# Attention and a gated feed-forward on one core: another plan of issue, transfers in parts, another order of the first steps

## The chip, the core and the metric

The kernel runs on one core of one Trainium2 chip. TensorE (PE), VectorE (DVE), ScalarE (ACT) and GpSimd (POOL) each work through their own queue of instructions in order. SyncE (SP) issues all the transfers, in order too. The metric is the device time of one execution in microseconds.

## The reference

There are 8 batches of 8 heads, 1152 keys and values of 64 numbers each, and queries that are averaged in pairs, so 576 per head. The attention's output, heads side by side, is the token matrix x of a gated feed-forward.

```python
q_pool = q.reshape(B, H, S // 2, 2, D).mean(axis=3)
scores = scale * np.matmul(q_pool, k.transpose(0, 1, 3, 2))
attn = np.exp(scores - np.max(scores, axis=-1, keepdims=True))
x = (attn / (attn.sum(-1, keepdims=True) + 1e-09)) @ v     # heads joined: B x 576 x 512
xk = mu_k * x + (1.0 - mu_k) * x_prev                       # x_prev: the token before
xr = mu_r * x + (1.0 - mu_r) * x_prev
k = np.maximum(xk @ w_k, 0.0)
out = 1.0 / (1.0 + np.exp(-(xr @ w_r))) * (k * k @ w_v)
```

## The kernel before

**Work.** A head's 576 queries are taken as 6 blocks of 96, 384 blocks in all. A block is a chain over four engines. PE multiplies 9 pieces of keys (`ks1`) by the block's queries into one of three score tiles `s` (L391). DVE takes a maximum over the pieces, `mx` (L398), PE turns it (L401), DVE takes it over the rest, `mb` (L404), PE spreads it (L406), and ACT writes it as one more row into the low half of the turned queries `qT` (L409). Nine products with `ks2` add the low halves and subtract the maximum (L415). ACT takes exp into `pf` (L421), POOL cuts out its low half `pl` (L423). Windows of 128 queries are then multiplied by the values `vt` and `vb` (L441, L443, L448).

**Preparation.** Every operand is split into a high and a low float16 half. For each head, `prep` loads `kr` and `vr` (L339), makes `kn` (ACT L346, DVE L348), turns it with a transposing transfer into `ks1` (L352), copies half of that to `ks2` (L354), and makes `vt` and `vb`. For each pair of heads, `queries` loads `qr` (L315), adds neighbours into `qs` (L319), makes the high and low halves of `qn` (ACT L322, DVE L326) and turns them into `qT` with one transposing transfer (L329). `qr`, `qs` and `qn` have one buffer, `qT` has two. `weights` loads 20 tiles into `st` (L499) and converts each with three operations on DVE (L511, L512, L514), two on ACT and one on POOL. A load of keys or values is 288 KB, of queries 576 KB, of a weight tile 512 KB.

**Feed-forward.** Tiles of 256 tokens. `mix` makes `xk` and `xr` from the tokens `xt` and the vectors `mu` and `omu` = 1 - mu (L549, L552, L557). PE multiplies by the weights (L577). The first such tile can start when batch 0, the first 48 blocks, is done.

**The order of work.** All of this is first recorded in a list: engine, planned duration, what is read and written. `Issue.run` then plays the list with these durations (`play`), engine by engine, in 1 + 6 rounds, keeps the order of the round with the shortest planned total, and writes the instructions in that order. Each engine later follows its own order, whatever the real times are. Transfers are one engine, "DMA", with a planned issue time (0.82 for a load, 1.01 for `ks1`, 1.9 for `qT`, 1.46 for a weight tile) and a fixed 2.0 from there to landing. Everything that stands ahead of the list (constants, memsets, `mu`) is ordered by the framework.

Of the kernel before, what the change touches and what calls it, by code (L numbers as in the profile page):

```python
# [19 lines left out]
P = 128  # L20
# [25 lines left out]


class Issue:
# [20 lines left out]
    def add(self, eng, dur, fn, r=(), w=(), key=0.0, port=None):  # L69
# [23 lines left out]
        self.ops.append((eng, dur, fn, key, deps, eng == "POOL" if port is None else port))  # L93
# [79 lines left out]
    def run(self, wait, rounds=6):  # L173
# [11 lines left out]
        start, total = self.play(eng, dur, pred, succ, [o[3] for o in ops], wait, port)  # L185
        best = (total, start)
        for _ in range(rounds):
            fin = [-(start[n] + dur[n]) for n in range(N)]
            back, _ = self.play(eng, dur, succ, pred, fin, wait, port)
            pr = [-(back[n] + dur[n]) for n in range(N)]  # L190
            start, total = self.play(eng, dur, pred, succ, pr, wait, port)
            if total < best[0]:
                best = (total, start)
        start = best[1]
        for n in sorted(range(N), key=lambda n: (start[n], n)):
# [4 lines left out]
def kernel(  # L200
# [109 lines left out]
    def queries(n, key):  # L310
# [18 lines left out]
        op("DMA", 1.9, lambda: nc.sync.dma_start_transpose(qT[i].rearrange("p r j x -> p (r j) x"),  # L329
                                                           qn[0].rearrange("p r j x -> p (r j x)")),  # L330
           r=[(m, j0) for m in ("qn", "qnl") for j0, _ in JS],
           w=[(m, i, hh, jj) for m in ("qT", "qTl") for hh in (0, 1) for jj in range(NB)], key=key + 2)

    def prep(n, key):
# [3 lines left out]
        def dma(o, src, buf):  # L338
            op("DMA", 0.82, lambda: nc.sync.dma_start(o, src), w=[buf], key=key - 2 * NB * PER)  # L339
# [3 lines left out]
        for c0, c1 in ((0, 5), (5, NC)):  # L343
# [21 lines left out]
        op("POOL", NC * D * 0.0009 + 0.066, lambda: nc.gpsimd.tensor_scalar(  # L365
# [6 lines left out]
    def block(n, j, i, t):  # L372
# [5 lines left out]
        kh, kl = ("qT", qi, hp, j), ("qTl", qi, hp, j)  # L378
# [332 lines left out]
```

## Time and profile before

| | |
|---|---|
| median of 3 runs | 1202.83 us (1202.06 to 1205.6) |
| profiled execution, its span | 1203.16 us, 1201.2 us |
| busy in the span: PE, DVE, ACT, POOL | 1133.2, 926.0, 834.6, 518.2 us |
| transfers: bytes, share of the 16 engines | 126.66 MB, 44.2% for the kernel's own queue |

The time of an execution lies some 2 us above its span, which goes from the first to the last instruction. A busy figure is the union of an engine's instructions. That PE is busy for 94% of the span is a mean over a start with hardly any work for it and a long rest in which it hardly stops, so stages are read apart below.

### The profile page before, as it was taken

What the parts mean: (1) busy time and instruction counts of PE and PEld (TensorE: products, weight loads), DVE (VectorE), ACT (ScalarE), POOL (GpSimd) and SP (SyncE); (2) the same over time, 40 slices, a digit from 0 to 9 for tenths busy, and PEclk for the clock granted to TensorE, in tenths of its full rate; (3) what the DMA queues carried; (4) which work ended last, traced back from release to release, by engine and by line L of the source; (5) the groups of instructions that cost most, each with busy time, mean ns of one, the idle gap of its engine ahead of it and who ended that gap; (6) DMA issues with size and microseconds to landing.
All of it is one profiled execution on the core that took longest, in us unless ns stands there. A gap on an engine that the chain in (4) does not pass through costs nothing.

```text
span 1201.2 us, 45386 instructions
## 1 busy us (share of the span) xinstructions
PE 1133.2 (94%) x19504; PEld 931.6 (78%) x19504; DVE 926.0 (77%) x1829; ACT 834.6 (69%) x1673; POOL 518.2 (43%) x547
## 2 busy tenths in 40 slices
PE   2778799999999999999999999999999999999998
PEld 2667787878788787978888887978787878888555
DVE  7798989888878778788787877886978788775431
ACT  5677777777667767677767676676767777755543
POOL 3555563534444444445444453544344444433111
PEclk9899999999999999999999999999999999999999
DMA  9676656564454443545443544545544544210000
GB/s 259 144 183 158 164 118 133 145 139 90 104 120 93 108 94 90 114 113 122 95 116 79 129 90 102 135 86 110 109 100 103 111 99 91 56 39 2 28 18 27
DMA packets 220777, 126.66 MB, mean 105 GB/s; under 512 B 156064, under 2 KB 192928, under 8 KB 220576
## 3 DMA queue, kind: packets, MB, share of 16 engines
q1 hardware_dynamic: 220576, 123.77, 44.2%
q8 instruction: 152, 2.49, 0.8%
q14 instruction: 49, 0.40, 0.1%
HBM read 67.11 MB, written 9.44 MB: 64 GB/s over the span
## 4 chain that ended last, share of the span: by engine, by line
PE 73%; ACT 10%; DMA 7%; issue 5%; DVE 5%; POOL 0%; SPq 0%; ACTq 0%; DVEq 0%; POOLq 0%
PE f L577 28%; PE s L415 10%; PE s L391 9%; PE a L448 6%; PE a L441 5%; PE a L443 5%; DMA qT<-qn 4%; PE s L577 4%; ACT pf L421 4%; PE a L577 2%; DVE mx L398 1%; PE s L401 1%; ACT qT L409 1%; PE s L406 1%; PE a L478 1%
## 5 line engine op out<-in xcount | busy, mean ns | idle before, releaser
L423 POOL TENSOR_SCALAR pl<-pf 128x864 f16<-128x864 uint16 x384 | 370.6, 965 | 463.3 <-ACT pf L421 430.6
L398 DVE TENSOR_REDUCE mx<-s 128x96 f16<-128x864 f32 x384 | 401.5, 1053 | 103.3 <-PE s L391 79.1
L421 ACT ACTIVATE pf<-s 128x864 int32<-128x864 f32 x384 | 336.7, 890 | 107.5 <-PE s L415 83.3
L391 PE MATMUL s<-qT,ks 128*128 128x96 f16 x3456 | 216.4, 207 | 33.2 <-DMA qT<-qn 17.1
L441 PE MATMUL a<-vt,pf 128*128 128x65 f16 x2880 | 235.5, 194 | 1.6 <-ACT pf L421 0.9
L443 PE MATMUL a<-vt,pf 128*128 128x64 f16 x2880 | 235.7, 194 | 0.0
L415 PE MATMUL s<-qT,ks 128*128 128x96 f16 x3456 | 214.4, 208 | 20.0 <-ACT qT L409 18.6
L391 PEld LDWEIGHTS <-ks 128*128 128x128 f16 x3456 | 184.1, 99 | 58.2 <-issue 23.2
L415 PEld LDWEIGHTS <-ks 128*128 128x128 f16 x3456 | 183.3, 99 | 48.9 <-issue 31.0
L441 PEld LDWEIGHTS <-pf 128*128 128x128 f16 x2880 | 203.9, 99 | 8.5 <-ACT pf L421 1.1
L443 PEld LDWEIGHTS <-pf 128*128 128x128 f16 x2880 | 193.8, 98 | 11.4 <-issue 0.9
L409 ACT ACTIVATE qT<-s 1x96 f16<-1x96 f32 x384 | 91.8, 242 | 108.8 <-PE s L406 98.7
L448 PE MATMUL a<-vb,pl 128*128 128x65 f16 x2880 | 154.3, 194 | 0.3 <-POOL pl L423 0.3
L404 DVE TENSOR_REDUCE mb<-s 96x1 f16<-96x128 f32 x384 | 108.5, 284 | 56.8 <-PE s L401 53.5
L577 PE MATMUL f<-xk,wk_lo 128*128 128x256 bf16 x496 | 136.9, 276 | 0.0
L577 PE MATMUL f<-xk,wk_hi 128*128 128x256 bf16 x496 | 136.6, 275 | 0.2 <-ACT r L604 0.2
L577 PE MATMUL f<-xlk,wk_hi 128*128 128x256 f16 x496 | 134.5, 271 | 0.0
L608 POOL TENSOR_TENSOR gl<-g 128x512 f16<-128x512 f32 x72 | 77.7, 1079 | 125.6 <-ACT g L606 124.2
L448 PEld LDWEIGHTS <-pl 128*128 128x128 f16 x2880 | 122.9, 99 | 4.9 <-POOL pl L423 0.4
L577 PEld LDWEIGHTS <-wk_hi 128*128 128x128 f16 x1152 | 104.8, 97 | 13.0 <-issue 0.4
L577 PE MATMUL f<-wv_hi,g 128*128 128x512 f16 x240 | 90.9, 379 | 1.1 <-ACT em L627 0.8
L577 PE MATMUL f<-wv_lo,g 128*128 128x512 f16 x240 | 90.9, 379 | 0.0
(89 smaller groups left out, 1881.7 us busy)
## 6 DMA issues: line engine op xcount, KB each, us to landing
qr<-in_q_dram SPq DMA_DIRECT2D x32, 576.0 KB, 4.7
kr<-in_k_dram SPq DMA_DIRECT2D x64, 288.0 KB, 3.2
vr<-in_v_dram SPq DMA_DIRECT2D x64, 288.0 KB, 3.0
ks<-ks SPq DMA_DIRECT2D x64, 144.0 KB, 2.7
out_dram<-em SPq DMA_DIRECT2D x36, 256.0 KB, 2.4
st<-in_moe_w_k_dram SPq DMA_DIRECT2D x8, 512.0 KB, 5.2
st<-in_moe_w_v_dram SPq DMA_DIRECT2D x8, 512.0 KB, 4.2
st<-in_moe_w_r_dram SPq DMA_DIRECT2D x4, 512.0 KB, 5.0
```

The costliest lines, as they stand in the source:

```text
L391: nc.tensor.matmul(cols(c, c + 1), ks1[hp][:, c, :], qhi, start=(c == c0), stop=False, skip_group_check=True)
L398: op("DVE", 0.967, lambda: nc.vector.tensor_reduce(mxz, grid(0, NC).rearrange("p c q -> p q c"), axis=AX.X, op=ALU.max), r=[("s", z)], w=[ ...
L404: op("DVE", 0.199, lambda: nc.vector.tensor_reduce(mbz[0:QN], s[0:QN, 0:P], axis=AX.X, op=ALU.max), r=[("s", z)], w=[("mb", z)], key=t + O ...
L409: op("ACT", 0.133, lambda: nc.scalar.activation(qlo[QN:QN + 1], s[QN:QN + 1, 0:QN], AF.Prelu, scale=1.0 - EPS, alpha=(1.0 + EPS) / (1.0 - ...
L415: nc.tensor.matmul(cols(c, c + 1), ks2[hp][:, c, :], qlo, start=False, stop=True, skip_group_check=True)
L421: op("ACT", NC * QN / 1200 + 0.051, lambda: nc.scalar.activation(pf[:, :, rows], grid(0, NC), AF.Exp, bias=SHIFT, scale=0.125 / (2.0 * SQ) ...
L423: op("POOL", NC * QN / 1000 + 0.066, lambda: nc.gpsimd.tensor_scalar(pl[:, :, rows], half(pf, U16, 0)[:, :, rows], LO, 1.0, op0=ALU.mult, ...
L441: nc.tensor.matmul(a_b[:, a0:a0 + VN], half(pf, F16, 1)[:, c, rows], vt[jv][:, c, D:D + VN], start=(w == 0 and c == 0), stop=False, skip_g ...
L443: nc.tensor.matmul(a_b[:, a0:a0 + D], half(pf, F16, 1)[:, c, rows], vt[jv][:, c, 0:D], start=False, stop=False, skip_group_check=True)
L448: nc.tensor.matmul(a_b[:, a0:a0 + VN], pl[:, c, rows], vb[jv][:, c, 0:VN], start=False, stop=(c == NC - 1), skip_group_check=True)
L577: nc.tensor.matmul(ps, terms[i][0], terms[i][1], start=(first and i == 0), stop=(i == last), skip_group_check=True)
L608: op("POOL", 2 * n * 0.0022 + 0.066, lambda f2=f2: nc.gpsimd.tensor_tensor(gl[:, f2, 0:n], g32[:, f2, 0:n], gh[:, f2, 0:n], op=ALU.subtrac ...
```

## The change

It has four parts. The planner: other durations take the place of the old ones, each transfer gets its own time from issue to landing (`tail`), every engine but PE is planned 8% slower (`LATE`) and each dependence between engines 0.1 us longer (`SLACK`), and a round's order is valued by a second pass that keeps it fixed (`follow`), over 12 rounds. The transfers: the load of `qr` and the turning of `ks1` are cut in two, the turning of `qT` in four (high and low half, pieces 0 to 4 and 5 to 8). The first steps: `mu` is recorded in the list after the first heads, the first two weight tiles wait for the first heads, two small copies of the identity move from DVE to POOL, a memset gets smaller, a one-element exp is written ahead of the list. The subtractions for keys and tokens are on DVE in both kernels.

```diff
+LATE, SLACK = 0.08, 0.1
...
-            lat = 0.0 if war and e == eng else self.lat(e, eng)
+            lat = self.ops[m][6] if e == "DMA" else 0.0 if war and e == eng else self.lat(e, eng)
...
-    def run(self, wait, rounds=6):
+    def run(self, wait, rounds=12):
...
-        dur = [o[1] for o in ops]
+        dur = [o[1] if o[0] == "PE" else o[1] * (1.0 + LATE) for o in ops]
...
+                lat += SLACK if eng[m] != eng[n] or eng[n] == "DMA" else 0.0
...
+            order = sorted(range(N), key=lambda n: (start[n], n))
+            start, total = self.follow(eng, dur, pred, succ, order, port)
+            if best is None or total < best[0]:
+                best = (total, order)
...
-    nc.vector.tensor_copy(identb, ident)
+    nc.gpsimd.tensor_copy(identb, ident)
...
-    nc.vector.tensor_scalar(negi, ident, -1.0 / SM, None, op0=ALU.mult)
+    nc.gpsimd.tensor_scalar(negi, ident, -1.0 / SM, 1.0, op0=ALU.mult, op1=ALU.mult)
...
+    nc.scalar.activation(mx[0][0:1, 0:1], identb[0:1, 0:1], AF.Exp)
...
-        nc.sync.dma_start(t_, m.rearrange("(c p) -> p c", p=P))
...
+        op("DMA", 0.46, lambda: nc.sync.dma_start(t_, m.rearrange("(c p) -> p c", p=P)), w=[("mu", n)], key=60.0)
+        op("DVE", 0.1, lambda: nc.vector.tensor_scalar(o, t_, -1.0, 1.0, op0=ALU.mult, op1=ALU.add),
...
-        op("DMA", 0.82, lambda: nc.sync.dma_start(qr[0], qv), w=[("qr",)], key=key - 2 * NB * PER)
...
+            op("DMA", 0.36, lambda js=js: nc.sync.dma_start(qr[0][:, js], qv[:, js]), w=[("qr", j0)],
+               key=key - 2 * NB * PER, tail=3.0)
...
-        op("DMA", 1.9, lambda: nc.sync.dma_start_transpose(qT[i].rearrange("p r j x -> p (r j) x"),
...
+            for r_, m, t_ in ((0, "qn", "qT"), (1, "qnl", "qTl")):
+                op("DMA", 0.14 * (j1 - j0) + 0.08, lambda js=js, r_=r_: nc.sync.dma_start_transpose(
+                    qT[i][:, r_, js], qn[0][:, r_, js].rearrange("p j x -> p (j x)")),
...
-        op("DMA", 1.01, lambda: nc.sync.dma_start_transpose(ks1[i], kn[i].rearrange("p c x -> p (c x)")),
...
+            op("DMA", 0.14 * (c1 - c0) + 0.08, lambda cs=cs: nc.sync.dma_start_transpose(
+                ks1[i][:, cs], kn[i][:, cs].rearrange("p c x -> p (c x)")),
...
-                op("DMA", 1.46, lambda s3=s3, src=wv[c, :, f:f + 512]: nc.sync.dma_start(s3, src), w=[ks], key=key)
+                op("DMA", 0.36, lambda s3=s3, src=wv[c, :, f:f + 512]: nc.sync.dma_start(s3, src),
+                   r=[("ks1", 1, 0), ("ks2", 0), ("vr", 1)] if iss.nw <= 2 else [], w=[ks], key=key, tail=4.5)
```

The change moves nearly every instruction of every queue, so three places are shown. The first is SP's queue at the start of the program, before the change:

```order
L293 DMA mu_k_132<-in_moe_mu_k_dram 128x4x1
L293 DMA mu_r_136<-in_moe_mu_r_dram 128x4x1
L315 DMA qr0_74<-in_q_dram 128x9x128
L339 DMA kr0_70<-in_k_dram 128x576
L339 DMA vr0_72<-in_v_dram 128x576
L339 DMA kr1_71<-in_k_dram 128x576
L339 DMA vr1_73<-in_v_dram 128x576
L499 DMA st1_120<-in_moe_w_k_dram 128x1024
L315 DMA qr0_74<-in_q_dram 128x9x128
L499 DMA st0_119<-in_moe_w_k_dram 128x1024
L352 DMA_TRANSPOSE ks1_0_79<-kn0_76 128x9x128
L329 DMA_TRANSPOSE qT0_83<-qn0_78 128x18x128
```

And SP's queue at the same place after it (lines of the changed kernel: L364 loads `qr`, L390 `kr` and `vr`, L340 `mu`, L404 turns `ks1`, L380 turns `qT`):

```order
L390 DMA kr0_70<-in_k_dram 128x576
L364 DMA qr0_74<-in_q_dram 128x5x128
L390 DMA kr1_71<-in_k_dram 128x576
L364 DMA qr0_74<-in_q_dram 128x4x128
L390 DMA vr0_72<-in_v_dram 128x576
L390 DMA vr1_73<-in_v_dram 128x576
L340 DMA mu_k_147<-in_moe_mu_k_dram 128x4x1
L340 DMA mu_r_149<-in_moe_mu_r_dram 128x4x1
L404 DMA_TRANSPOSE ks1_0_79<-kn0_76 128x5x128
L404 DMA_TRANSPOSE ks1_0_79<-kn0_76 128x4x128
L364 DMA qr0_74<-in_q_dram 128x5x128
L380 DMA_TRANSPOSE qT0_83<-qn0_78 128x5x128
```

Keys now come first, `mu` comes seventh and eighth, the weight tiles (`st`) stand further down, and the first turned queries are 5 pieces instead of 18.

The second place is DVE's queue after the memsets, before the change:

```order
L319 TENSOR_TENSOR qs0_75<-qr0_74 128x320
L319 TENSOR_TENSOR qs0_75<-qr0_74 128x256
L326 SCALAR_TENSOR_TENSOR qn0_78<-qs0_75,qn0_78 128x5x64
L348 TENSOR_TENSOR kn0_76<-kr0_70,kn0_76 128x5x64
L348 TENSOR_TENSOR kn0_76<-kr0_70,kn0_76 128x4x64
L254 CAST identb_66<-ident_61 128x128
L256 TENSOR_SCALAR negi_68<-ident_61 128x128
L326 SCALAR_TENSOR_TENSOR qn0_78<-qs0_75,qn0_78 128x4x64
```

And after it (L399 is the keys' subtraction, L341 makes `omu`):

```order
L399 TENSOR_TENSOR kn0_76<-kr0_70,kn0_76 128x5x64
L366 TENSOR_TENSOR qs0_75<-qr0_74 128x320
L399 TENSOR_TENSOR kn0_76<-kr0_70,kn0_76 128x4x64
L341 TENSOR_SCALAR omu_k_148<-mu_k_147 128x4
L341 TENSOR_SCALAR omu_r_150<-mu_r_149 128x4
L399 TENSOR_TENSOR kn1_77<-kr1_71,kn1_77 128x5x64
L373 SCALAR_TENSOR_TENSOR qn0_78<-qs0_75,qn0_78 128x5x64
L366 TENSOR_TENSOR qs0_75<-qr0_74 128x256
```

The two `omu` rows, which read the seventh and eighth transfer, now stand ahead of the low halves of the second head's keys and of the queries.

The third place is ACT's queue after some 140 blocks, where `qn` for the next pair of heads is written, before the change:

```order
L359 ACTIVATE vt2_87<-vr0_72 128x5x64
L359 ACTIVATE vt2_87<-vr0_72 128x4x64
L322 ACTIVATE qn0_78<-qs0_75 128x640
L409 ACTIVATE qT0_83<-s0_127 1x96
L421 ACTIVATE pf_91<-s2_129 128x9x96
L421 ACTIVATE pf_91<-s0_127 128x9x96
L322 ACTIVATE qn0_78<-qs0_75 128x512
```

And the write of `qn` for the same pair after it (L369 is `qn`, L463 the row of `qT`, L475 `pf`, L604 `mix`):

```order
L604 ACTIVATE tmp1_114<-xt1_103,omu_r_150 128x128
L369 ACTIVATE qn0_78<-qs0_75 128x640
L463 ACTIVATE qT1_84<-s0_127 1x96
L412 ACTIVATE vt1_86<-vr1_73 128x5x64
L412 ACTIVATE vt1_86<-vr1_73 128x4x64
L463 ACTIVATE qT1_84<-s1_128 1x96
L475 ACTIVATE pf_91<-s0_127 128x9x96
```

A block's row of `qT` stands right behind the write of `qn` in both; where the write stands was set before with 1.9 + 2.0 us for the transfer that must have read `qn`, now with 0.64 to 0.78 + 2.0 us for a part of it.

## Rows read from the trace of the kernel before

**Rows 1.** Busy time of each engine by stage: stretch, length, engines, granted clock, DMA.
```profile
0.00:17.09 17.09, 0.00 (x1) 0.10 (x1) 12.73 (x36) 6.88 (x14) 4.84 (x10) 1.00 0.89 253
17.09:156.30 139.21, 107.83 (x2232) 98.17 (x2232) 120.94 (x235) 100.09 (x196) 74.45 (x79) 0.94 0.69 169
156.30:161.90 5.60, 4.42 (x117) 4.10 (x114) 4.88 (x10) 4.68 (x10) 3.09 (x4) 1.00 0.76 171
161.90:1201.20 1039.30, 1020.93 (x17167) 829.26 (x17163) 787.41 (x1551) 722.97 (x1454) 435.83 (x456) 1.00 0.41 94
```
**Rows 2.** Timeline of the first 18 us: start, duration, engine, line; idle before it.
```profile
0.74 0.46 SPq L293 DMA_DIRECT2D mu_k<-in_moe_mu_k_dram  x1
1.80 0.50 SPq L315 DMA_DIRECT2D qr<-in_q_dram  x1
...
6.92 1.28 ACT L322 ACT_TABLE_LOAD   x1 [6.92 <-DVE qs L319]
...
12.23 3.43 SPq L329 DMA_TRANSPOSE qT<-qn  x1
...
17.09 2.32 PE L391 MATMUL s<-qT,ks 128*128 128x96 f16 x27 [17.09 <-DMA qT<-qn]
```
**Rows 3.** As rows 1, two stretches of 2 us at the start.
```profile
2.00:4.00 2.00, 0.00 (x0) 0.00 (x0) 0.84 (x3) 0.00 (x0) 1.19 (x2) 1.00 0.50 51
6.00:8.00 2.00, 0.00 (x0) 0.00 (x0) 1.09 (x12) 1.08 (x1) 0.10 (x1) 1.00 1.05 387
```
**Rows 4.** ACT's waits from 17 to 162 us: total, times, longest, in us.
```profile
ACT f L509 <- DMA st<-in_moe_w_k_dram: 5.7, 2, 3.0
```
**Rows 5.** Timeline around 90 us.
```profile
89.55 0.62 ACT L509 ACTIVATE f<-st 128x512 f32<-128x512 f32 x1 [2.59 <-DMA st<-in_moe_w_r_dram]
...
90.49 0.32 PE L415 MATMUL s<-qT,ks 128*128 128x96 f16 x2 [1.98 <-ACT qT L409]
```
**Rows 6.** Timeline from 156 to 162 us, up to the first feed-forward product.
```profile
156.34 0.47 DVE L552 SCALAR_TENSOR_TENSOR xk<-xt,mu_k,tmp 128x256 f32<-128x256 f32 x1
...
157.17 0.54 PE L415 MATMUL s<-qT,ks 128*128 128x96 f16 x9
...
159.91 1.31 PE L391 MATMUL s<-qT,ks 128*128 128x96 f16 x27
...
161.88 0.28 PE L577 MATMUL f<-xk,wk_hi 128*128 128x256 bf16 x1
```
**Rows 7.** Waits from 161.9 us on: total, times, longest, in us.
```profile
ACT qn L322 <- DMA qT<-qn: 14.6, 13, 2.5
PE s L415 <- ACT qT L409: 9.0, 19, 1.8
```
**Rows 8.** Timeline around 425 us.
```profile
418.70 3.33 SPq L329 DMA_TRANSPOSE qT<-qn  x1
...
425.55 0.74 ACT L322 ACTIVATE qn<-qs 128x640 f16<-128x640 f32 x1 [1.45 <-DMA qT<-qn]
...
426.61 0.54 PE L415 MATMUL s<-qT,ks 128*128 128x96 f16 x9 [1.84 <-ACT qT L409]
```
**Rows 9.** Transposing transfers by line: issue in ns, minimum/median/maximum; time to landing.
```profile
L329 SPq DMA_TRANSPOSE qT<-qn x32: 2674/3315/7428, 12.2 to 1036.2; - x32
...
DMA to landing us min/median/max: 4.7/5.8/11.8
...
L352 SPq DMA_TRANSPOSE ks<-kn x64: 1242/1298/2642, 10.7 to 1063.9; - x64
...
DMA to landing us min/median/max: 3.2/3.2/5.4
```
**Rows 10.** DVE's groups from 0 to 162 us: busy us, mean ns; idle before, releasers.
```profile
L398 DVE TENSOR_REDUCE mx<-s 128x96 f16<-128x864 f32 x56 | 57.9, 1049 | 7.3 <-PE s L391 3.3 <-ACT qT L409 1.8 <-PE s L406 1.7
L404 DVE TENSOR_REDUCE mb<-s 96x1 f16<-96x128 f32 x54 | 15.0, 282 | 6.2 <-PE s L401 5.8
...
L512 DVE SCALAR_TENSOR_TENSOR f<-st,f 128x512 int32<-128x512 int32 x20 | 13.7, 686 | 0.1
```

More of the change, by code (lines that the diff above doesn't have):

```diff
@@ L92, in add @@
                 self.rd.setdefault(b, []).append(n)
-        self.ops.append((eng, dur, fn, key, deps, eng == "POOL" if port is None else port))
+        self.ops.append((eng, dur, fn, key, deps, eng == "POOL" if port is None else port, tail))
     @staticmethod
@@ L171, in play, with follow @@
         return start, max(free.values())
-    def run(self, wait, rounds=6):
+    @staticmethod
+    def follow(eng, dur, pred, succ, order, port):
+        N = len(eng)
+        ready, left = [0.0] * N, [len(p) for p in pred]
+        start = [0.0] * N
+        queue, at, free = {}, {}, {}
+        for n in order:
+            queue.setdefault(eng[n], []).append(n)
+        for e in queue:
+            at[e], free[e] = 0, 0.0
+        way, total = 0.0, 0.0
+        for _ in range(N):
+            best = None
+            for e, q in queue.items():
+                if at[e] < len(q):
+                    n = q[at[e]]
+                    if not left[n]:
+                        t = max(free[e], ready[n], way if port[n] else 0.0)
+                        if best is None or t < best[0]:
+                            best = (t, e, n)
+            t, e, n = best
+            start[n] = t
+            end = t + dur[n]
+            at[e] += 1
+            free[e] = end
+            if port[n]:
+                way = end
+            total = max(total, end)
+            for m, lat in succ[n]:
+                if ready[m] < end + lat:
+                    ready[m] = end + lat
+                left[m] -= 1
+        return start, total
+    def run(self, wait, rounds=12):
         ops = self.ops
@@ L182, in run @@
             for m, lat in o[4].items():
+                lat += SLACK if eng[m] != eng[n] or eng[n] == "DMA" else 0.0
                 pred[n].append((m, lat))
                 succ[m].append((n, lat))
-        start, total = self.play(eng, dur, pred, succ, [o[3] for o in ops], wait, port)
-        best = (total, start)
+        start, _ = self.play(eng, dur, pred, succ, [o[3] for o in ops], wait, port)
+        best = None
         for _ in range(rounds):
+            order = sorted(range(N), key=lambda n: (start[n], n))
+            start, total = self.follow(eng, dur, pred, succ, order, port)
+            if best is None or total < best[0]:
+                best = (total, order)
             fin = [-(start[n] + dur[n]) for n in range(N)]
@@ L190, in run @@
             pr = [-(back[n] + dur[n]) for n in range(N)]
[L191 to L195, printed above, removed]
+            start, _ = self.play(eng, dur, pred, succ, pr, wait, port)
+        self.total = best[0]
+        for n in best[1]:
             ops[n][2]()
@@ L328, in queries @@
                r=[("qs", j0), ("qn", j0)], w=[("qnl", j0)], key=key + 2, port=True)
-        op("DMA", 1.9, lambda: nc.sync.dma_start_transpose(qT[i].rearrange("p r j x -> p (r j) x"),
-                                                           qn[0].rearrange("p r j x -> p (r j x)")),
-           r=[(m, j0) for m in ("qn", "qnl") for j0, _ in JS],
-           w=[(m, i, hh, jj) for m in ("qT", "qTl") for hh in (0, 1) for jj in range(NB)], key=key + 2)
+            blocks = [(hh, jj) for hh in (0, 1) for jj in range(NB)
+                      if hh * TQ + jj * QN < j1 * P and hh * TQ + (jj + 1) * QN > j0 * P]
+            for r_, m, t_ in ((0, "qn", "qT"), (1, "qnl", "qTl")):
+                op("DMA", 0.14 * (j1 - j0) + 0.08, lambda js=js, r_=r_: nc.sync.dma_start_transpose(
+                    qT[i][:, r_, js], qn[0][:, r_, js].rearrange("p j x -> p (j x)")),
+                   r=[(m, j0)] + ([("qn", j0)] if r_ else []), w=[(t_, i, hh, jj, j0) for hh, jj in blocks],
+                   key=key + 2, tail=2.0)
     def prep(n, key):
@@ L377, in block @@
         qhi, qlo = (qT[qi][:, r].rearrange("p j x -> p (j x)")[:, q0:q0 + QN] for r in (0, 1))
-        kh, kl = ("qT", qi, hp, j), ("qTl", qi, hp, j)
+        kh, kl = ([(t_, qi, hp, j, j0) for j0, j1 in ((0, 5), (5, NQ)) if q0 < j1 * P and q0 + QN > j0 * P]
+                  for t_ in ("qT", "qTl"))
         s = s_b[z]
@@ L395, in block @@
             op("PE", (c1 - c0) * 0.043, lambda c0=c0, c1=c1: scores(c0, c1),
-               r=[("ks1", hp), kh], w=[("s", z)], key=t)
+               r=[("ks1", hp, c) for c in (0, 5) if c < c1 and (c0 < 5 or c)] + kh, w=[("s", z)], key=t)
         op("DVE", 0.967, lambda: nc.vector.tensor_reduce(mxz, grid(0, NC).rearrange("p c q -> p q c"),
@@ L600, in ff @@
                               (wlo["k"][:, c, fs], hk[:, c, 0:n], r)]
-                products(pv[:, f - f0], pk, terms, n / 2400.0 + 0.0025, first=(f == f0))
+                products(pv[:, f - f0], pk, terms, n / 2400.0 + 0.005, first=(f == f0))
             z = turn("r32")
```

38 lines of the change are left out of this document (20 added, 18 removed).

## The prediction

> **What bounds the kernel now.** I first read the busy time by stage [rows 1], because the 94% of PE over the span hides two kernels in one. From 161.9 us on, PE is busy for 1020.9 of 1039.3 us, so it is the bound there and only 18.4 us can be had, some of it the end after the last product. Before 161.9 us PE is busy for 107.8 + 4.4 = 112 us. There is no feed-forward work yet, since the first product of it needs all of batch 0, and the attention alone does not fill PE. DVE is the busiest engine of this stage: 12.7 us in the first 17.09, then 120.9 of 139.2. So the first 162 us are set by how much DVE has to do before batch 0 is ready, plus the time in which DVE stands still: 4.4 + 18.3 = 22.7 us up to 156.3 us, where the fourth piece of `xk` [rows 6], the last that the first feed-forward tile needs, starts on DVE.
>
> Next I read what DVE and PE wait for. The timeline of the start [rows 2] shows the first product at 17.09 us, released by the one transfer that turns `qT`, issued at 12.23 us. Ahead of it stand two `mu` issues (`qr` starts at 1.80 us, the first issue at 0.74) and a table load of 1.28 us that ACT begins only when `qs` is there. In the early stage the waits of ACT name weight tiles that have not landed [rows 4], and the timeline shows what follows: at 89.55 us ACT has stood 2.59 us in front of a weight tile, a row of `qT` waits behind it in ACT's queue, and PE stands 1.98 us [rows 5]. DVE's own idle time is mostly that in front of `mx` and `mb`, 13.5 us [rows 10], that is, of work that such a chain holds up.
>
> In the late stage [rows 7] the largest wait of PE is that for ACT's row of `qT`, 9.0 us. One cause of it stands in the row above: ACT waits 14.6 us, 13 times, to write `qn`, until the transfer of the pair before has read it. Around 425 us one sees a whole case [rows 8]: `qT` issued at 418.70 for 3.33 us, ACT held until 425.55, PE idle for 1.84 us.
>
> **The change part by part.** *Start.* The bytes flow from about 4 us, at 387 GB/s once they do [rows 3]. In the new order nothing stands ahead of the first keys, so I let the flow begin 1.06 us sooner (1.80 - 0.74), at 3. Up to `vr0` 1440 KB go in order, 3.7 us, so `vr0` is there at some 6.7; ACT's first `qn` stands behind one `vt`, which needs it, and is done near 8. Turning 5 of 18 pieces takes 3.43 x 5/18 = 0.95 us to issue and some 2.4 to land, so the first product stands near 11 us instead of 17. The table load is off this path, since ACT now loads before its first wait. Against that, `mu` is seventh and eighth in a full queue. It lands behind 1.73 MB, near 8 us, and the two `omu` rows hold DVE's queue, with the low halves of the second head's keys and of the queries behind them. DVE would reach these rows near 6, so some 2.2 us are lost. How a part is priced rests on rows 9: `ks1` with 9 pieces lands 3.2 - 1.3 = 1.9 us and `qT` with 18 lands 5.8 - 3.3 = 2.5 us after an issue that grows with the pieces [rows 9]. The Trainium skill's page DMA: Bandwidth & Descriptors (Anatomy of one DMA) knows only a fixed 2.0 us and 436 GB/s, by which 5 pieces of 32 KB would land 2.4 us after the issue begins, as an estimate, the first product near 10 us, and the sum 1 us lower; the measured issue decides.
>
> *DVE's work before the feed-forward.* I counted both orders up to the fourth `xk` on DVE. There are three blocks fewer ahead of it (51 for 54), 3 x (1.049 + 0.284) = 4.0 us, one weight tile more, 3 x 0.69 = 2.1 us [rows 10], and four smaller operations fewer, of which two are the copies of the identity that POOL now makes, where it idles. These four are worth between nothing and 2.8 us. I take 1. DVE's work falls from 133.7 to about 130.7 us.
>
> *DVE's idle time.* The first 17.09 us held 4.4; I put 3.5 for the new start (0.9 before its first memset, 0.4 before the first keys, 2.2 for `mu`). Of the 18.3 us after that I take half off, 9 remain: the planner now counts 4.5 us until a weight tile has landed where it counted 2.0, so it issues earlier or uses it later, and loads are not queued as 0.82 or 1.46 us of a busy engine. Bounds: 5 if every wait behind a transfer goes, all 18 if the full queues make them. Sum: 130.7 + 3.5 + 9 = 143 us for the fourth `xk`, 139 to 152. The first feed-forward product stood 5.5 us behind it [rows 6]. In the new order only 51 blocks of scores stand ahead of it on PE instead of 55.5, so I take 4: 147 us instead of 161.9, between 141 and 158. That is **-14.9 us**, bounds -21 and -4.
>
> *What PE then still owes.* 222 products fewer stand ahead of the first feed-forward product: 81 of scores, 135 with values, 6 others. A product of 96 columns takes (1.31 - 0.54) / 18 = 0.043 us [rows 6], one of 65 columns about two thirds, 0.03, the others at most 0.05. That is 3.5 + 4.1 + 0.3 = **+8 us**, which come later on an engine that is full.
>
> *Late stage.* The transfer that turned `qT` was planned at 1.9 + 2.0 us and took 5.8 to land [rows 9]; its parts are planned at 0.64 to 0.78 + 2.0, and the issue rate of 3.3 us for 18 pieces, 0.18 a piece, bears that out for the part itself. So the planner now places the write of `qn` behind the real landing, and a half of `qn` waits for its own half alone. I take about half of the 9.0 us off for it. The rest, and the other small waits, are where the extra 8% and 0.1 us help: an order that is right by less than that falls over on the chip. PE idles 18.4 us here; I take **-8 us**, bounds 0 (as much is lost elsewhere in an order that is new everywhere) and -12 (all but the end).
>
> *At nothing.* There are 192 transfers more (32 for `qr`, 96 for `qT`, 64 for `ks1`), each with an issue of 0.1 to 0.4 us on SP. SP has the time, since DMA's share is 0.41 here; without that cover the 96 and 64 would cost 0.1 each, 16 us in the queue of one engine. The memset on POOL and the one-element exp stand beside waits for the first loads. The subtractions on DVE don't move to another engine.
>
> Sum: -14.9 + 8 - 8 = -14.9 us on the profiled 1203.16 us; the median is 0.3 below that, so **1188 us**.
>
> **The rivals.** *The early gain alone.* The late order loses as much in new places as it wins at `qn`: 1202.8 - 6.9 = 1196 us. For it speaks that 14.6 us of ACT's waits cost PE only a part of 9.0, so the rest is chance meetings, and they are dealt anew.
>
> *More than this.* DVE idles 5 us, PE loses 6 us late: -21 + 8 - 12 = -25, 1178 us. For it speaks that the named waits are all of one kind, a planned time that was too short.
>
> *The parts gain nothing.* In the first 17 us DMA's share is 0.89 and early on 0.69, so a part lands no sooner than the whole did, the start wins 2 us less, DVE idles 15 us instead of 9, and -6.9 becomes +1; with half the late gain that is 1200 us, inside what a measurement tells from no change (0.3%, 3.6 us either way). The Trainium skill's page DMA: Bandwidth & Descriptors (Rules for kernel authors) speaks for this one: it wants many small transfers joined into one. The Trainium skill's page Perfetto Trace Analysis (DMA Optimizations) says that splitting helps where the engines are mostly idle; by the trace that is the late stage, not the start.
>
> *Slower: DVE stands still as long as before.* The planner knows no bandwidth. With a queue that is full at the start, each planned landing is too early, an in-order engine stops at it, and this time `mu`, then second-half keys, stand in DVE's own queue. With 25 us of idle time the fourth `xk` is at 156 and the first product at 160: -2 + 8 = +6, 1209 us, if the late stage gives nothing. It decides from a first product later than 154 us (147 + 6.9) plus what the late stage gives back.
>
> **How the numbers follow.** My forecast has 0.52, the early gain alone 0.17, more than this 0.12, no gain from the parts 0.09, slower 0.10. Faster by over 0.3%: 0.52 + 0.17 + 0.12 = 0.81. The same: 0.09. Slower: 0.10. The range is 1175 to 1202 us: it holds the first four but for their ends and leaves out the slower case; the forecast's own range is 1181 to 1195.
>
> **What would show it.** The first product near 11 us, with a DVE wait of about 2 us at `omu` behind `mu`. DVE idle by 13 us, not 23, ahead of the fourth `xk`. The first feed-forward product near 147 us. From there on PE idle for 10 us instead of 18, and the wait of ACT's `qn` for `qT` nearly gone. The prediction is wrong if the first feed-forward product comes after 154 us, or if the same sum of small waits stands late under other names.

## The result, and the profile after

The changed kernel takes **1189.56 us** (median of 4 runs, 1186.88 to 1192.27) where the kernel before took 1202.49 beside it: a ratio of 0.9887, 95% interval 0.9858 to 0.9916. Forecast were 1188 us and "faster" at 0.81. The profiled execution took 1192.27 us, its span 1190.5. One execution of one kernel below (`a_qt2`) took 1431.7 us at a mean granted clock of 0.755 and is left out of its times. The size came as forecast; the place did not. The changed kernel is cut below at its own two boundaries (first product, first feed-forward product); the rows are to be set against [rows 1], whose second and third row, taken together, stand on top here:

```profile
17.09:161.90 144.81, 112.26 (x2343) 102.27 (x2343) 125.82 (x244) 104.77 (x205) 77.55 (x83) 0.94 0.70 169
```
```profile
0.00:13.20 13.20, 0.00 (x0) 0.10 (x1) 8.47 (x27) 5.60 (x12) 3.34 (x11) 1.00 0.90 206
13.20:164.00 150.80, 109.04 (x2120) 98.54 (x2120) 123.16 (x238) 99.78 (x195) 73.73 (x76) 0.89 0.75 166
164.00:1190.50 1026.50, 1017.97 (x17387) 834.34 (x17384) 801.84 (x1564) 733.81 (x1468) 450.76 (x463) 1.00 0.43 96
```

The first feed-forward product did not come sooner at all: 164.0 us for 161.9, with 2120 products ahead of it for 2342 (the 2343 of the row take in that product itself). So the early stage, which was to bring 14.9 us, lost 2.1, and with less done. The late stage, which was to bring 8 us and to pay 8 for the products that moved into it, is 12.8 us shorter (1039.3 to 1026.5) with 220 products more in it.

**The start.** The timeline of the changed kernel's first 14 us answers to [rows 2]:

```profile
0.73 1.28 ACT L397 ACT_TABLE_LOAD   x1 [0.73 <-PEq L752]
0.74 0.40 SPq L390 DMA_DIRECT2D kr<-in_k_dram  x1
...
5.30 3.37 SPq L404 DMA_TRANSPOSE ks<-kn  x2
...
8.50 0.72 ACT L369 ACTIVATE qn<-qs 128x640 f16<-128x640 f32 x1
...
9.14 0.17 DVE L341 TENSOR_SCALAR omu_k<-mu_k 128x4 f32<-128x4 f32 x1 [3.13 <-DMA mu_k<-in_moe_mu_k_dram]
...
9.39 1.22 SPq L380 DMA_TRANSPOSE qT<-qn  x1
...
13.20 1.04 PE L445 MATMUL s<-qT,ks 128*128 128x96 f16 x11 [13.20 <-DMA qT<-qn]
```

The table load is off the path, and the first product moved from 17.09 to 13.20 us. DVE stands 3.13 us at `omu` behind `mu`, as foreseen but for 0.9 us. What was not foreseen is the length of the transposing issues: 3.37 us for the two parts of `ks1`, 1.22 for 5 pieces of `qT`.

**The parts.** The instructions of the two lines that turn `qT` and `ks1` in the changed kernel (issue in ns, minimum/median/maximum, then the time to landing) answer to [rows 9]:

```profile
L380 SPq DMA_TRANSPOSE qT<-qn x128: 1189/1236/4547, 9.4 to 1023.7; - x128
...
DMA to landing us min/median/max: 2.4/3.1/9.2
```
```profile
L404 SPq DMA_TRANSPOSE ks<-kn x128: 1194/1217/2648, 5.3 to 1052.6; - x128
...
DMA to landing us min/median/max: 2.4/2.6/6.9
```

A part of 4 or 5 pieces costs SP 1.2 us, hardly less than the 1.3 us that 9 pieces cost whole. The plan has 0.64 to 0.78. The parts do land sooner (3.1 us for 5.8, 2.6 for 3.2).

**An early stall.** The timeline of the changed kernel from 70 to 86 us shows one case of what such a difference adds to, and the windows around it show PE's clock:

```profile
70.12 1.78 SPq L404 DMA_TRANSPOSE ks<-kn  x1
...
71.99 3.85 SPq L380 DMA_TRANSPOSE qT<-qn  x3
...
72.70 0.54 PE L445 MATMUL s<-qT,ks 128*128 128x96 f16 x9
...
76.59 1.66 SPq L553 DMA_DIRECT2D st<-in_moe_w_r_dram  x1
...
78.30 0.42 SPq L390 DMA_DIRECT2D kr<-in_k_dram  x1
...
82.25 0.76 ACT L397 CAST kn<-kr 128x320 f16<-128x320 f32 x2 [6.85 <-DMA kr<-in_k_dram]
...
83.33 0.48 PE L469 MATMUL s<-qT,ks 128*128 128x96 f16 x4 [7.24 <-ACT qT L463]
...
83.82 0.70 DVE L566 TENSOR_SCALAR f<-f 128x512 int32<-128x512 int32 x1 [5.75 <-ACT f L564]
...
84.75 0.88 PE L469 MATMUL s<-qT,ks 128*128 128x96 f16 x9 [0.35 <-ACT qT L463]
```
```profile
70.00:76.00 6.00, 3.95 (x67) 3.09 (x65) 6.00 (x13) 4.87 (x9) 4.37 (x5) 1.00 1.07 156
76.00:87.00 11.00, 3.37 (x44) 2.98 (x42) 4.32 (x10) 4.40 (x9) 2.72 (x4) 0.53 0.76 188
87.00:95.00 8.00, 7.41 (x199) 7.01 (x195) 7.18 (x15) 5.16 (x11) 4.55 (x5) 1.00 0.40 99
```

Three parts of `qT` hold SP for 3.85 us (planned at 3 x 0.64 to 0.78 and 8% on top, so 2.1 to 2.5), and a part of `ks1` ahead of them 1.78. The load of `kr` stands behind them and behind two more issues, and goes out at 78.30. Not all of that is the price of the parts: one of the two issues, that of a weight tile, took 1.66 us, where the plan has 0.36. ACT's write of `kn` waits 6.85 us for it; a row of `qT` and a weight tile wait behind that in ACT's queue; so PE stands 7.24 us and DVE 5.75.

**The late stage.** Two rows of PE's waits from 164 us on answer to [rows 7]:

```profile
PE s L445 <- ACT pf L475: 1.8, 5, 0.7
...
PE s L469 <- ACT qT L463: 0.7, 2, 0.5
```

Of 9.0 us for ACT's row of `qT`, 0.7 are left, and no wait of ACT's `qn` for the transfer (14.6 us before) stands in the list any more.

### The profile page after: what moved, and what is told of

Same layout as the page of the kernel before. It is cut to its first block, busy times and chain, and to the rows that moved or that the text cites. A ratio compares the mean times of both kernels' runs of the same rounds, so it can differ in the third digit from the quotient of the medians.

```text
span 1190.5 us, 45818 instructions
## 1 busy us (share of the span) xinstructions
PE 1127.0 (95%) x19504; PEld 933.0 (78%) x19504; DVE 933.5 (78%) x1827; ACT 839.2 (70%) x1674; POOL 527.8 (44%) x549
## 4 chain that ended last, share of the span: by engine, by line
PE 85%; DVE 5%; ACT 4%; DMA 3%; issue 2%; SPq 0%; POOL 0%; ACTq 0%; DVEq 0%
PE f L632 33%; PE s L445 11%; PE s L469 11%; PE a L502 7%; PE a L495 7%; PE a L497 7%; PE s L632 4%; DVE mx L452 2%; ACT pf L475 2%; PE s L455 2%; PE a L632 2%; PE s L460 1%; PE a L532 1%; DMA qT<-qn 1%; DMA vr<-in_v_dram 1%
## 5 line engine op out<-in xcount | busy, mean ns | idle before, releaser
L477 POOL TENSOR_SCALAR pl<-pf 128x864 f16<-128x864 uint16 x384 | 379.1, 987 | 445.3 <-ACT pf L475 429.1
L475 ACT ACTIVATE pf<-s 128x864 int32<-128x864 f32 x384 | 337.5, 890 | 103.2 <-PE s L469 81.6
L445 PE MATMUL s<-qT,ks 128*128 128x96 f16 x3456 | 222.4, 208 | 29.2 <-ACT pf L475 14.7
L469 PE MATMUL s<-qT,ks 128*128 128x96 f16 x3456 | 218.8, 209 | 14.6 <-ACT qT L463 11.3
L463 ACT ACTIVATE qT<-s 1x96 f16<-1x96 f32 x384 | 92.5, 243 | 104.3 <-PE s L460 94.1
L632 PE MATMUL f<-wv_hi,gl 128*128 128x512 f16 x240 | 90.9, 379 | 0.0
```

Source lines behind the costliest of these rows:

```text
L445: nc.tensor.matmul(cols(c, c + 1), ks1[hp][:, c, :], qhi, start=(c == c0), stop=False, skip_group_check=True)
L463: op("ACT", 0.133, lambda: nc.scalar.activation(qlo[QN:QN + 1], s[QN:QN + 1, 0:QN], AF.Prelu, scale=1.0 - EPS, alpha=(1.0 + EPS) / (1.0 - ...
L469: nc.tensor.matmul(cols(c, c + 1), ks2[hp][:, c, :], qlo, start=False, stop=True, skip_group_check=True)
L475: op("ACT", NC * QN / 1200 + 0.051, lambda: nc.scalar.activation(pf[:, :, rows], grid(0, NC), AF.Exp, bias=SHIFT, scale=0.125 / (2.0 * SQ) ...
L477: op("POOL", NC * QN / 1000 + 0.066, lambda: nc.gpsimd.tensor_scalar(pl[:, :, rows], half(pf, U16, 0)[:, :, rows], LO, 1.0, op0=ALU.mult, ...
L632: nc.tensor.matmul(ps, terms[i][0], terms[i][1], start=(first and i == 0), stop=(i == last), skip_group_check=True)
```

## The experiments

Each was timed in five rounds beside the kernel before on the same chip; ratios are to that. To compare stages of orders that put different amounts ahead of the first feed-forward product, I take 0.036 us a product (the prediction's 8 us for 222): "early" is how much later that product comes than at 161.9 us, plus 0.036 us for each of the 2343 products that no longer stand ahead of it; "late" is how much longer the stage from there to the end is than 1039.3 us, less the same amount. The two add up to the difference of the profiled spans. Both come from the windows of each run's trace at its own boundaries, whose rows stand below where they carry a verdict; PE's idle time is a stretch less its busy time. The trace of `a_jit` is of its fastest execution, 6.1 us under its median, so its row shows less loss than its ratio.

| kernel | median us | ratio | first ff at | products ahead | PE idle before it, after it | early | late |
|---|---|---|---|---|---|---|---|
| before | 1201.8 to 1203.5 | 1 | 161.9 | 2343 | 49.6, 18.4 | 0 | 0 |
| changed | 1189.6 | 0.9887 | 164.0 | 2120 | 55.0, 8.5 | +10.1 | -20.8 |
| a_noslack | 1202.2 | 1.0002 | 164.8 | 2275 | 50.3, 15.5 | +5.3 | -6.7 |
| b_slack | 1181.1 | 0.9806 | 160.8 | 2355 | 47.0, 8.3 | -1.5 | -21.8 |
| b_times | 1193.6 | 0.9929 | 164.1 | 2503 | 45.4, 15.3 | -3.6 | -5.8 |
| b_times_slack | 1174.7 | 0.9765 | 154.5 | 2326 | 49.0, 10.3 | -6.8 | -19.4 |
| b_times_slack_jit | 1179.6 | 0.9809 | 152.6 | 2089 | 46.7, 9.5 | -0.2 | -19.7 |
| a_whole | 1179.0 | 0.9808 | 160.7 | 2292 | 46.4, 6.5 | +0.6 | -24.5 |
| whole_jit | 1180.6 | 0.9805 | 162.2 | 2391 | 46.5, 7.4 | -1.4 | -24.4 |
| a_parts122 | 1177.8 | 0.9791 | 157.5 | 2297 | 45.5, 9.7 | -2.7 | -22.0 |
| a_parts122_jit | 1182.5 | 0.9821 | 172.2 | 2445 | 44.9, 6.3 | +6.6 | -26.1 |
| a_jit | 1194.7 | 0.9930 | 161.1 | 2270 | 47.8, 13.1 | +1.8 | -16.5 |
| a_jit2 | 1190.1 | 0.9895 | 173.0 | 2385 | 53.1, 6.3 | +9.6 | -24.9 |
| a_qt2 | 1179.7 | 0.9804 | not taken | | | | |

### Is it the room in the plan?

*a_noslack*: the changed kernel, without the 8% and the 0.1 us.

```diff
-LATE, SLACK = 0.08, 0.1
+LATE, SLACK = 0.0, 0.0
```

> The changed kernel with LATE and SLACK at zero; all else is kept. Theory 1: the late gain (PE's waits after the first feed-forward product, 18.4 us before and 8.5 us after) comes from the room that the plan leaves, so most of it goes, and the time is near 1199 us, with 16 us or more of idle PE late. Theory 2: it comes from the transfers' true times and parts, so the time stays within 3 us of 1189.6. Theory 3: every new order is dealt anew, and the time lands anywhere from 1180 to 1206.

Measured: 1202.15 us, ratio 1.0002 (0.9985 to 1.0019). The whole gain is gone. *b_slack* is the reverse: the kernel before, with its old durations, whole transfers and old first steps, and only the room, the second pass and the 12 rounds.

```diff
+LATE, SLACK = 0.08, 0.1
...
-        dur = [o[1] for o in ops]
+        dur = [o[1] if o[0] == "PE" else o[1] * (1.0 + LATE) for o in ops]
...
+                lat += SLACK if eng[m] != eng[n] or eng[n] == "DMA" else 0.0
...
+            start, total = self.follow(eng, dur, pred, succ, order, port)
```

> The kernel before with the planner's room alone: LATE 0.08, SLACK 0.1, the second pass and 12 rounds; the old durations, whole transfers, the old first steps. If room alone makes the late gain (theory 1), PE's losses after the first feed-forward product fall by some 10 us and the time is near 1191 us. If the room only works on true times (rival), the waits of ACT to write qn stay at 15 us or more and the time is within 4 us of 1202. If only the deal matters, anywhere from 1185 to 1206.

Measured: 1181.08 us, ratio 0.9806 (0.9785 to 0.9828), 8 us better than the whole change and 10 better than was expected if room alone makes the late gain. The windows of a_noslack, then of b_slack:

```profile
10.98:164.80 153.82, 114.52 (x2275) 102.30 (x2275) 131.18 (x252) 105.07 (x207) 77.08 (x81) 0.89 0.73 171
164.80:1199.80 1035.00, 1019.46 (x17234) 830.35 (x17231) 793.28 (x1555) 727.62 (x1457) 437.87 (x458) 1.00 0.44 95
```
```profile
17.07:160.80 143.73, 113.85 (x2355) 103.85 (x2355) 128.47 (x247) 106.29 (x210) 78.95 (x81) 0.93 0.71 175
160.80:1177.90 1017.10, 1008.77 (x17153) 824.72 (x17150) 792.97 (x1548) 723.06 (x1450) 442.19 (x457) 1.00 0.42 96
```

The late stage of b_slack, with 14 products fewer than before, is 22.2 us shorter; that of a_noslack 4.3. PE's idle time there is 8.3 against 15.5 us. The second pass and the 12 rounds were not run by themselves, but a_noslack has them too, and no such gain. Over the 13 kernels of the table that have windows, the late column is -16.5 to -26.1 in the ten with room and 0 to -6.7 in the three without. So it is the room. Its two numbers were not tried apart.

*b_times*: the kernel before with the measured durations and landing times alone, no room.

```diff
-        op("DMA", 1.9, lambda: nc.sync.dma_start_transpose(qT[i].rearrange("p r j x -> p (r j) x"),
+        op("DMA", 3.3, lambda: nc.sync.dma_start_transpose(qT[i].rearrange("p r j x -> p (r j) x"),
...
-                op("DMA", 1.46, lambda s3=s3, src=wv[c, :, f:f + 512]: nc.sync.dma_start(s3, src), w=[ks], key=key)
+                op("DMA", 0.36, lambda s3=s3, src=wv[c, :, f:f + 512]: nc.sync.dma_start(s3, src), w=[ks], key=key, tail=4.5)
```

> The kernel before with nothing but the trace's times in its plan: every transfer's issue and landing, and four durations on PE and POOL; whole transfers, no room in the plan, the old first steps and the old choice of a round. Theory 1: ACT's 14.6 us of waiting to write qn go, worth some 5 us, the small waits stay: near 1197 us. Theory 2: all of the late gain is there, and the time is at or below 1190 us. Theory 3: anywhere from 1180 to 1206.

Measured: 1193.55 us, ratio 0.9929 (0.9905 to 0.9953), between its two theories. *b_times_slack* is both, still with whole transfers and the old first steps.

> The kernel before with true times and room together, but whole transfers and the old first steps. Theory 1 (room works late, parts cost early, first steps are worth little): near 1181 us, within 4 us of the kernel with whole transposing transfers (1179). Rival, the first steps and the load of qr in parts matter: 1186 us or more.

Measured: 1174.73 us, ratio 0.9765 (0.9749 to 0.978), the fastest of all and 6 us under what was expected. The windows of b_times, then of b_times_slack:

```profile
19.43:164.10 144.67, 118.74 (x2503) 107.75 (x2502) 133.19 (x260) 108.84 (x214) 82.03 (x86) 0.94 0.71 173
164.10:1191.80 1027.70, 1012.43 (x17007) 823.04 (x17003) 780.80 (x1535) 717.53 (x1442) 440.00 (x451) 1.00 0.41 94
```
```profile
20.55:154.50 133.95, 105.50 (x2326) 95.98 (x2327) 125.58 (x242) 103.13 (x204) 78.56 (x81) 0.99 0.73 180
154.50:1175.00 1020.50, 1010.22 (x17182) 827.27 (x17179) 789.05 (x1554) 721.99 (x1455) 450.17 (x456) 1.00 0.43 96
```

Measured times alone bring 8.5 us, over both stages; PE's idle time late stays at 15.3 us. b_times_slack has its first product at 20.55 us, 7 us later than the changed kernel, and its first feed-forward product 9.5 us sooner. What the measured times add to the room (1181.1 us without them, 1174.7 and, in another order below, 1179.6 with them) is no more than two orders of one plan differ by.

### Is it the parts?

*a_whole*: the changed kernel with `ks1` and `qT` each one transfer again, at measured times.

```diff
-            for r_, m, t_ in ((0, "qn", "qT"), (1, "qnl", "qTl")):
-                op("DMA", 0.14 * (j1 - j0) + 0.08, lambda js=js, r_=r_: nc.sync.dma_start_transpose(
...
+        op("DMA", 3.3, lambda: nc.sync.dma_start_transpose(qT[i].rearrange("p r j x -> p (r j) x"),
...
-            op("DMA", 0.14 * (c1 - c0) + 0.08, lambda cs=cs: nc.sync.dma_start_transpose(
...
+        op("DMA", 1.3, lambda: nc.sync.dma_start_transpose(ks1[i], kn[i].rearrange("p c x -> p (c x)")),
```

> The changed kernel with ks1 and qT turned by one transfer each again (planned with the trace's 1.3 and 3.3 us of issue); first steps, times and room in the plan are kept. Theory 1: a transposing transfer holds SP some 1.2 us however few its pieces, so the parts ate the early gain; SP's issue time for them falls from 343 to about 200 us, the first feed-forward product comes near 155 us instead of 164, and the time is near 1182 us, with the late stage as in the changed kernel. Theory 2: the parts made the late gain, so ACT's wait to write qn comes back and the time rises to 1195 or more. Theory 3: anywhere from 1180 to 1206.

Measured: 1179.04 us, ratio 0.9808 (0.9779 to 0.9838). So the parts as planned cost some 10 us, though the first feed-forward product came at 160.7 us and not near 155 as theory 1 has it. That can be their load, 343 us of SP's time for 195 (256 issues of 1.2 us and more for 96 of 1.3 to 3.3), or the price that the plan has for them. *a_parts122* leaves all the parts and corrects the price.

```diff
-                op("DMA", 0.14 * (j1 - j0) + 0.08, lambda js=js, r_=r_: nc.sync.dma_start_transpose(
+                op("DMA", 1.22, lambda js=js, r_=r_: nc.sync.dma_start_transpose(
...
-            op("DMA", 0.14 * (c1 - c0) + 0.08, lambda cs=cs: nc.sync.dma_start_transpose(
+            op("DMA", 1.22, lambda cs=cs: nc.sync.dma_start_transpose(
```

> The changed kernel with its transposing parts planned at the 1.22 us of issue that the trace shows, instead of 0.64 to 0.78. If the false price in the plan was what the early stage lost, the time falls to 1183 us or less. If the parts' own load on SP's queue was it, the time stays within 4 us of 1189.6.

Measured: 1177.78 us, ratio 0.9791 (0.9774 to 0.9807), level with a_whole. The windows of a_parts122, then of a_whole:

```profile
11.67:157.50 145.83, 111.99 (x2297) 101.80 (x2297) 131.97 (x249) 105.25 (x206) 77.46 (x81) 0.92 0.81 180
157.50:1176.50 1019.00, 1009.35 (x17213) 826.86 (x17209) 796.77 (x1556) 725.66 (x1457) 441.59 (x457) 1.00 0.46 96
```
```profile
16.84:160.70 143.86, 114.33 (x2292) 103.56 (x2292) 128.85 (x247) 106.56 (x208) 77.58 (x81) 0.92 0.74 179
160.70:1177.30 1016.60, 1010.12 (x17218) 827.55 (x17214) 801.88 (x1552) 724.23 (x1455) 454.27 (x458) 1.00 0.42 96
```

The parts stand on SP for as long as in the changed kernel (medians of 1216 and 1239 ns, 128 of each), but the plan now knows it, and PE's idle time ahead of the first feed-forward product falls from 55.0 to 45.5 us. *a_qt2* has the middle way: `ks1` whole, `qT` in two halves of 9 pieces at 1.3 us, the time that 9 pieces of `ks1` take.

```diff
-                op("DMA", 0.14 * (j1 - j0) + 0.08, lambda js=js, r_=r_: nc.sync.dma_start_transpose(
+            op("DMA", 1.3, lambda r_=r_: nc.sync.dma_start_transpose(
```

> ks1 whole, qT in two transfers of 9 pieces (high and low half) planned at 1.3 us each. If the issue of a part costs 1.2 us up to 9 pieces, two halves take SP 2.5 us where the whole took 3.3 and the high half lands 2.5 us sooner: SP's issue time for transposing near 165 us, and the time 2 to 4 us below the whole one's 1179, near 1176. If the price is per piece, 195 us and 1179.

Measured: 1179.7 us, ratio 0.9804 (0.9786 to 0.9822), some 4 us above what was expected; no better than whole or in four parts. What SP spent on the halves is open.

### How much is the luck of the order?

Another number anywhere in the plan gives another order of the whole program, so a single pair of times may differ by that alone. *a_jit* and *a_jit2* are the changed kernel with 8.5% and 7.5% for its 8%; *a_parts122_jit*, *whole_jit* and *b_times_slack_jit* are the kernels above with 8.5%.

```diff
-LATE, SLACK = 0.08, 0.1
+LATE, SLACK = 0.085, 0.1
```

> A control: the changed kernel with LATE at 0.085 instead of 0.08, which changes nothing but the deal of the order. Theories 1 and 2: within 3 us of 1189.6, with 7 to 11 us of idle PE late. Theory 3: it differs from 1189.6 by 5 us or more.

> The changed kernel with the room per operation set to 0.075 in place of 0.08: another order of the same work, with the parts still planned at 0.64 to 0.78 us. Theory (the price that the plan has for the parts costs about 10 us in the early stage): 1187 to 1195 us, as the two orders before it with that price (1189.6 and 1194.7). Rival (only which order the planner happens to find): anywhere from 1175 to 1195, so below 1183 speaks for it.

> The changed kernel with its parts planned at 1.22 us, and the room per operation set to 0.085 in place of 0.08: another order. Theory (the true price gives the 10 us): 1178 plus or minus 5. Rival (only the order that happens to be found): 1189 or more is as likely as 1178.

> The changed kernel with both transposing transfers whole again, at their measured times, and the room per operation set to 0.085 in place of 0.08: another order. Theory (it is the parts at their false price that cost): 1179 plus or minus 5. Rival (only the order that happens to be found): 1189 or more is as likely.

> The kernel before with the trace's times and the room in its plan, whole transfers and the old first steps, the room per operation set to 0.085 in place of 0.08: another order. Theory (the new first steps are worth nothing, since the early stage is held by VectorE and not by the first product): 1175 plus or minus 5, level with the changed kernel's whole transfers under their new first steps (1179). Rival (only the order that happens to be found): 1185 or more is as likely.

Measured: a_jit 1194.65 us, ratio 0.993 (0.9905 to 0.9955); a_jit2 1190.07, 0.9895 (0.9875 to 0.9916); a_parts122_jit 1182.48, 0.9821 (0.9799 to 0.9844); whole_jit 1180.62, 0.9805 (0.9783 to 0.9828); b_times_slack_jit 1179.6, 0.9809 (0.9786 to 0.9832). By its own words a_jit, 5.1 us off, speaks for its theory 3, an order dealt anew, and misses the other two. Between orders of one plan up to 5 us lie here. The three orders with the short price for the parts (1189.6, 1194.7, 1190.1) lie above the two with the measured price (1177.8, 1182.5) and the two with whole transfers (1179.0, 1180.6), and no interval of the first group touches one of the others. So the price costs about 11 us (means of 1191.5 and 1180.1), more than two or three orders of one plan differ by here. The parts at their measured price are worth nothing against whole transfers (1180.1 and 1179.8), and neither are the new first steps, together with the load of `qr` in two: with whole transfers 1179.8 with them, 1177.2 without, which the luck covers. The windows of a_jit2, then of a_parts122_jit:

```profile
11.40:173.00 161.60, 119.86 (x2385) 108.67 (x2385) 136.67 (x266) 109.51 (x215) 79.83 (x84) 0.92 0.73 168
173.00:1185.90 1012.90, 1006.61 (x17124) 824.53 (x17120) 781.97 (x1541) 719.85 (x1448) 438.13 (x454) 1.00 0.44 96
```
```profile
11.70:172.20 160.50, 127.34 (x2445) 115.08 (x2445) 138.02 (x267) 111.41 (x219) 83.32 (x86) 0.86 0.75 172
172.20:1181.70 1009.50, 1003.21 (x17060) 821.23 (x17059) 781.83 (x1539) 718.07 (x1444) 443.33 (x452) 1.00 0.45 96
```

The time at which the first feed-forward product comes says nothing by itself: in both it stands above 172 us, since more attention is done ahead of it. PE's idle time before it separates these two, 53.1 and 44.9 us. Over the orders with room it is 47.8 to 55.0 with the short price and 44.9 to 49.0 without, so the two ranges overlap by a_jit. What separates all the kernels with parts is how long ACT waits for transfers early on. The largest such waits of the changed kernel up to its first feed-forward product, then of a_parts122 (total, times, longest, in us):

```profile
ACT kn L397 <- DMA kr<-in_k_dram: 9.7, 3, 6.8
ACT vt L412 <- DMA vr<-in_v_dram: 5.7, 2, 4.0
```
```profile
ACT vt L412 <- DMA vr<-in_v_dram: 4.1, 2, 2.8
ACT kn L397 <- DMA kr<-in_k_dram: 2.2, 1, 2.2
```

Added up from 10 to 160 us, ACT's waits for transfers are 12.7 to 16.3 us in the four orders with the short price (a_noslack among them) and 6.9 and 5.1 in the two with the measured one; the two with whole transfers have 12.1 and 12.6, of which one wait to write `qn` is 6.6 or 6.7. So with the short price the transfers of these kernels come later than the order of ACT's queue was made for. By the means of the table, some 6 us of the price stand early and 3.5 late; what makes the late share, which is nearly all of a_jit's loss, was not followed.

## Why the prediction came right in size, and where its steps failed

**DVE's idle time ahead of the feed-forward: this step failed, and with it the early term of -14.9 us.** Half of 18.3 us was to go, 3.5 + 9 were to remain. DVE's work was sized well: 131.5 us until the fourth `xk` begins at 163.88, for 130.7. But DVE stood still for 163.88 - 131.5 = 32.4 us, 4.7 in the first 13.2 and 27.6 behind them, outside the bound of 18. The first feed-forward product came at 164.0, for 147. The path through the fourth `xk` was wrong as well: that `xk` takes 1.16 us, so the product, which reads the first piece alone, began before it was written, and in a_parts122, a_whole, a_jit and b_times_slack it stands ahead of it. The prediction's own sign of being wrong, a first product later than 154 us, was met: the place of the slower rival came true, without the loss that it forecast.

The price of the parts is only a share of this. Up to the fourth `xk` DVE is idle for 22.0 to 32.4 us in the four orders with the short price, for 16.3 to 27.1 in the eight without it, and for 22.6 in the kernel before. Not one comes near the 12.5 of the prediction. In the measure of the table its early forecast is -14.9 + 8 = -6.9; the changed kernel has +10.1, and the four orders with measured price or whole transfers +0.8 on the mean. So some 8 of the 17 us are missing at the right price too: that half of DVE's idle time would go has no run behind it, and what holds DVE up there besides the price stays open.

**"The issue rate of 3.3 us for 18 pieces, 0.18 a piece, bears that out for the part itself": this is the wrong step behind a part of it.** The price of a part was scaled from the whole by its pieces. The row beside it, `ks1` with 9 pieces in 1.30 us, is the nearer one for 5 pieces and was read as a point on a line. The part costs 1.2 us. With that the 0.64 to 0.78 of the new plan is a durations error of the same kind that the change takes away elsewhere; it cost 11 us (above). One case of how it does so is seen at 70 to 84 us, where SP falls behind its plan and the loads behind the parts with it; DVE's 5.75 us there are more than half of the 9.8 us by which its idle time grew. That all 11 us are of this kind was not followed through each order.

**192 transfers at nothing: right in effect, not in size.** With the price right the 160 of them that turn `ks1` and `qT` cost nothing that can be measured (a_parts122 against a_whole). But they take 148 us more of SP's time, 0.9 for each one added and not 0.1 to 0.4. SP has that time, as the prediction said, though the DMA share of 0.41 that it gave for it is that of the 16 DMA engines and not of SP's queue. The 32 of `qr` were not tried apart.

**The start.** The first product came at 13.20 us for 11: `vr0` and with it `qn` were later by some 1.2 us, and the part was again 1.22 us for 0.95. From the start of its issue to the first product 3.81 us passed (9.39 to 13.20), where the prediction's sum has 3.35 and the estimate beside it 2.4. It made no difference to the end: b_times_slack, whose first product comes at 20.55 us, has its first feed-forward product soonest but one, and the new first steps are worth nothing that can be measured.

**The 8 us still owed: right.** 2120 products stand ahead of the feed-forward, 222 fewer, and they come late.

**The late term of -8 us: right in its mechanism, far too small.** PE's idle time was to fall from 18 to 10 us, and fell to 8.5; the waits at `qn` and at ACT's row went as said. But the stage gave 20.8 us and not 8, and "only 18.4 us can be had" was wrong. At the median spacing of each kind of product in the trace, the 220 products more should have added 7.7 us to PE's busy time; it fell by 3.0 (1020.93 to 1017.97). So 10.7 us came out of time that the view counts as busy. Two rows of PE by line, from the kernel before and from the changed one, both of the late stage, tell how:

```profile
L415 PE MATMUL s<-qT,ks 128*128 128x96 f16 x2970 | 181.8, 206 | 10.1 <-ACT qT L409 9.0
```
```profile
L469 PE MATMUL s<-qT,ks 128*128 128x96 f16 x3000 | 186.3, 206 | 0.8 <-ACT qT L463 0.7
```

A product has 206 ns in both, yet follows the last one after 43 ns [rows 6]. So a stop of up to some 0.16 us between two products leaves no idle time at all, and a longer one shows 0.16 us too little. The Trainium skill's page Perfetto Trace Analysis (Tensor Engine Instruction) says that the end of a TensorE instruction in a profile is computed from its size and not observed; the trace agrees, with 206 ns in both kernels. The traces can be asked for these stops: the time by which products start later than the median spacing of their kind, as far as PE counts as busy meanwhile, adds up to 29.1 us in the late stage of the kernel before and to 18.4 in that of the changed one, again 10.7 less. Without the room it is 25.4 to 29.1 us (three kernels), with it 15.8 to 18.4 (ten), and stretches at the lower clock hold at most 1.6 of any of these sums. What brought the 20.8 us is the room, not the part: without it the late stage gives 6.7 (a_noslack), with it and whole transfers 21.8 (b_slack). The prediction gave "the extra 8% and 0.1 us" only a share of the rest.

**The sum.** -14.9 + 8 - 8 became +2.1 + 8 - 20.8 = -10.7 us in the span: an early term that was 17 us too good met a late one that was 12.8 us too small. That leaves the profiled execution 4.2 us above the forecast; the median is 1.6 above it, since it lies 2.7 under the profiled execution. That the two errors met so nearly is luck. None of the rivals was this case.

## What to carry to other kernels

An order that is planned from single durations fell over on small errors here: plan every engine but the one that bounds some per cent slower and every handover a little longer (8% and 0.1 us here; nothing beyond 7.5 to 8.5% was tried), and look for the gain in the stage where the busiest engine hardly ever seems idle, since small stops hide inside its busy time. Give a transfer cut in parts the issue time that such a part takes on the chip, not its share of the whole; a wrong price for 256 instructions cost more than the 256 instructions. A sum that comes out right does not show that its terms are: read each term at its own boundary. And before two planned orders are compared, take a second and third order of the same plan: here they differ by up to 5 us of 1180.

## What the runs showed of the hardware that was not expected

- The issue of a transposing transfer did not shrink with its pieces below 9: 1.22 us for 5 and for 4 (1.19 at the least in 256 issues), 1.30 for 9, 3.3 for 18.
- PE's granted clock fell to the lower of its two levels, 1.2 GHz, in the stretch in which PE stood: 0.53 on the mean from 76 to 87 us, where PE was busy for 3.37 of 11 us, and 1.00 from 87 on. Nine products that took 0.54 us at 72.70 took 0.88 at 84.75. Over the early stage the mean was 0.94 before, 0.89 after and 0.99 in b_times_slack, where 2326 products kept PE busy for 105.5 us, against 112.3 for 2343 before. So an early stall costs PE more than its own length, though how much of the end that moves was not measured.
